# First network in eight tiles of three units instead of six of two and four of three

## The chip, the core and the metric

The kernel runs on one core of one Trainium2 chip. The metric is the device time of one launch in microseconds (us); lower is better. Engines are named as in the profile: PE (TensorE matmul), PEld (its weight loads), DVE (VectorE), ACT (ScalarE), POOL (GpSimd) and SP (SyncE, which issues the DMAs here).

## What is computed

Three stages follow each other. An attention with a complex decay runs over 4 batches, 8 heads, 768 steps and 48 channels; its output, put side by side over the heads, is a matrix of 3,072 tokens by 384, which passes through two feed-forward networks:

```
for t in range(S):                       # attention, per batch and head
    S_re, S_im = ar * S_re - ai * S_im + k[t] v[t]^T, ar * S_im + ai * S_re
    y[t] = q[t] @ S_re
g = x @ w_gate; x = (silu(g) * (x @ w_val)) @ w_out          # first network, 1,536 wide
h = x @ w_in;   out = (h - tanh(h)) @ w2_out                 # second network, 2,048 wide
```

## The kernel before

**Units and groups.** The tokens fall into 24 units of 128 (six per batch). Two units form a group. `group_steps` (L271) makes the decay powers of a group: its inputs are normed one group ahead (L224 to L250), turned by PE (`put_a`, L252), multiplied up in 14 steps of `cstep` (L262; three DVE instructions each, L266, L268, L269), copied to `NW` by ACT (L312, L313) and finished in L345 to L351. `unit_a` (L357) turns q and k of a unit, multiplies them with `NW` (L370, L376) and sends them through a DRAM scratch (`qk_d`, L378 to L383). `unit_b` (L402) makes the scores (L420), the masked scores (L423 to L426), the carried state (L432 to L441), the output (L446, L448) and the turned output, split into a high and a low part, `xh` and `xl` (L461 to L464).

**First network.** `moe1_tile` (L526) takes a tile of units. For each of 12 slices `f` of the width it makes the gate and the value products (L554, 18 products of the slice's weights with all columns of the tile), SiLU on ACT (L558), their product on DVE (L563), its split by ACT and POOL (L514, L515), and one slice later the output products (L538, nine of them). So a tile has 12 x 27 = 324 products, each as wide as the tile: 256 columns for two units, 384 for three. L523 loads a slice of `w_out` again for each tile after the first. A tile can start when `xh` and `xl` of its last unit are there.

**Order.** Ahead of the first tile the program runs the attention of the units of that tile (L682) and decodes the first ten weight slices (`dec1`, L184). Then, after each half slice of tile `ti`, `bg` (L715) advances the attention by `RATE` = 6 steps until the units of the next tile are done (L704), and during tile 0 also decodes the other 14 weight slices. In the last tile (L707) no attention is left; the second network's weights are decoded there. The second network (`moe2_tile`, L607) has its own tiles of three units. A scheduler then puts each engine's instructions into an order of its own, by a simulated timeline; on the chip an engine takes them in that order.

```
TILES = (2, 2, 2, 2, 2, 2, 3, 3, 3, 3)                  # L58
while prog["done"] < TILES[0] - 1:                      # L682
    att_next(TILES[0] - 1, SHARE0)
...
goal = sum(TILES[:ti + 2]) - 1                          # L704
```

Of the kernel before, what the change touches and what calls it, by code (L numbers as in the profile page):

```python
# [41 lines left out]
def tile_kernel(ctx: ExitStack, tc: tile.TileContext, q, k, v, a_re, a_im, w_gate, w_val, w_out, w2_in, w2_out, out):  # L42
# [12 lines left out]
    NF1 = FF1 // P  # L55
    NF2 = FF2 // P

    TILES = (2, 2, 2, 2, 2, 2, 3, 3, 3, 3)  # L58

    RAW, MID = 2, 3  # L60

# [4 lines left out]
    N_A, N0, W2STEP, LON = 6, 20, 2, 10  # L66
    TU = max(TILES)
    N_EARLY = 2
# [103 lines left out]
    def dec1_load():  # L172
        if len(raws) < len(dec1_jobs):
            kind, f = dec1_jobs[len(raws)]
            r = raw_p.tile([P, 2, DM], I64, tag="raw", name="raw", bufs=RAW)
            if kind == "o":
                ins = SP.dma_start(out=r[:, 0], in_=w_out[f * P:(f + 1) * P, :])
            else:
                for c, src in enumerate((w_gate, w_val)):
                    ins = SP.dma_start(out=r[:, c].rearrange("p (k c) -> p k c", k=NJ), in_=src[:, f * P:(f + 1) * P].rearrange("(k p) c -> p k c", p=P))  # L180
            raws.append(r)
            raw_ins.append(ins.ins)
# [213 lines left out]
    tile_u0 = []  # L396
    for ti, n in enumerate(TILES):
        tile_u0.append(len(unit_tile))
# [121 lines left out]
    def load_wo(n):  # L520
        if NF1 <= n < NF1 * len(TILES):
            t = m1.tile([P, 2, DM], F32R, tag="wo", name="wo", bufs=3)
            SP.dma_start(out=t.bitcast(F32), in_=wo_d[n % NF1])  # L523
            wo_t[n] = t

    def moe1_tile(ti, bg):  # L526
        x = xt.pop(ti)
        n_t = TILES[ti] * P
        tok = tile_u0[ti] * P
# [136 lines left out]
    def att_next(goal, share):  # L666
        prog["n"] += 1
        if prog["done"] < goal:
            if next(ustream, None) == "wait":
                next(gstream, None)  # L670
                return
        else:
            prog["more"] = max(prog["more"], 1.0)
        prog["more"] += share
        while prog["more"] >= 1:
            prog["more"] -= 1
            group_next()

    load_a(0)
    for i in range(RAW):  # L680
        dec1_load()
    while prog["done"] < TILES[0] - 1:  # L682
        att_next(TILES[0] - 1, SHARE0)
        if prog["n"] == QAT:
# [216 lines left out]
```

## Time and profile before

| | |
|---|---|
| median of 3 runs (range) | 1281.08 us (1279.9 to 1281.22) |
| profiled execution, its own time | 1280.44 us |
| its span, first to last instruction | 1278.7 us |
| mean granted TensorE clock | 0.943 |
| busy: PE, DVE, ACT, POOL | 1147.8, 1008.1, 695.3, 465.8 us |

The time is that of the whole launch, the span that of the program's instructions; 1.74 us lie around it. Clock 1.0 is 2.4 GHz, 0.5 is 1.2 GHz; a figure between is a mean over a stretch. Matmuls overlap on PE, so that what one costs in a run of them is the distance from start to start, not its duration. A stretch of the program is read by cutting the span where a tile's first SiLU (L558) starts.

### The profile page before, as it was taken

How to read it: one execution, taken by the hardware profiler on the slowest of the kernel's cores; microseconds unless marked ns; L12 is line 12 of the kernel's file. 1: busy time of each engine (PE TensorE's matmuls, PEld its weight loads, DVE VectorE, ACT ScalarE, POOL GpSimd, SP SyncE). 2: the span in 40 equal slices, each digit the busy share in tenths (PEclk: the TensorE clock that was granted, in tenths of full speed). 3: DMA queues.
4: the chain of work that ended last, by engine and by line, in shares of the span. 5: the costliest groups of instructions: out<-in, count | busy, mean ns of one | idle time of the engine just before them, and what ended most of it. 6: DMA issues, size and time to landing. Idle time of an engine off the chain costs nothing.

```text
span 1278.7 us, 21147 instructions
## 1 busy us (share of the span) xinstructions
PE 1147.8 (90%) x7512; PEld 1113.6 (87%) x7512; DVE 1008.1 (79%) x1961; ACT 695.3 (54%) x1454; POOL 465.8 (36%) x402
## 2 busy tenths in 40 slices
PE   3346899898999999999999998987999999999997
PEld 2126888898999998999999998877999999999996
DVE  6988988697675849677683328999998899999996
ACT  6454655556545463736534224446666566666664
POOL 0034454333252223233232224544444444444442
PEclk9755979999899999999999999998999999999999
DMA  6586667679676776768565546752101101101000
GB/s 169 141 203 146 145 185 194 158 194 215 158 176 178 183 186 151 184 155 185 160 145 141 147 118 221 235 173 87 57 1 57 38 20 56 38 19 56 1 19 22
DMA packets 282289, 163.53 MB, mean 128 GB/s; under 512 B 155328, under 2 KB 263232, under 8 KB 282176
## 3 DMA queue, kind: packets, MB, share of 16 engines
q1 hardware_dynamic: 282176, 162.10, 48.7%
q8 instruction: 61, 1.00, 0.3%
q14 instruction: 52, 0.43, 0.1%
HBM read 121.26 MB, written 37.86 MB: 124 GB/s over the span
## 4 chain that ended last, share of the span: by engine, by line
PE 53%; DVE 23%; ACT 8%; DMA 8%; issue 4%; POOL 2%; SPq 1%; DVEq 0%; ACTq 0%; POOLq 0%
PE l L617 14%; PE l L635 13%; PE l L554 12%; PE acc L538 5%; PE psS L420 2%; DVE prod L266 2%; DVE t L143 2%; DMA TQ<-qk_d 2%; PE psY L448 2%; DVE PL L268 2%; PE psY L446 2%; DVE t L142 1%; DVE t L583 1%; DVE t L144 1%; DMA raw<-in_moe_w_val_dram 1%
## 5 line engine op out<-in xcount | busy, mean ns | idle before, releaser
L515 POOL TENSOR_TENSOR lo<-t,hi 128x384 fp32r<-128x384 f32 (+1 forms) x247 | 289.4, 1172 | 517.2 <-ACT hi L514 485.7
L554 PE MATMUL l<-x,wgv 128*128 128x256 f32 (+1 forms) x2160 | 366.8, 317 | 21.6 <-DVE t L563 14.6
L554 PEld LDWEIGHTS l<-x,wgv 128*128 128x128 f32 x2160 | 324.4, 197 | 29.4 <-DVE t L563 19.4
L514 ACT CAST hi<-t 128x384 fp32r<-128x384 f32 (+1 forms) x248 | 119.5, 482 | 244.4 <-DVE t L563 141.6
L635 PE MATMUL l<-x,wi 128*128 128x384 f32 x1152 | 223.0, 339 | 8.3 <-DVE t L584 7.2
L635 PEld LDWEIGHTS l<-x,wi 128*128 128x128 f32 x1152 | 202.5, 189 | 9.9 <-DVE t L584 8.3
L617 PE MATMUL l<-w,hi 128*128 128x384 f32 x768 | 188.0, 338 | 0.5 <-ACT hi L514 0.5
L538 PE MATMUL acc<-hi,wo 128*128 128x256 f32 (+1 forms) x720 | 180.0, 312 | 4.0 <-ACT hi L514 2.7
L583 DVE SCALAR_TENSOR_TENSOR t<-vv,t 128x384 f32<-128x384 f32 x128 | 139.8, 1092 | 11.8 <-DVE t L582 0.5
L617 PEld LDWEIGHTS l<-w,hi 128*128 128x128 f32 x768 | 139.5, 189 | 0.8 <-ACT hi L514 0.8
L538 PEld LDWEIGHTS acc<-hi,wo 128*128 128x128 f32 x720 | 127.0, 193 | 5.8 <-ACT hi L514 3.8
L617 PE MATMUL l<-w,lo 128*128 128x384 f32 x384 | 120.2, 337 | 0.0
L563 DVE TENSOR_TENSOR t<-t,l 128x256 f32<-128x256 f32 (+1 forms) x120 | 56.2, 468 | 81.0 <-PE l L554 67.8
L538 PE MATMUL acc<-lo,wo 128*128 128x256 f32 (+1 forms) x360 | 111.3, 315 | 3.8 <-POOL lo L515 3.8
L266 DVE TENSOR_TENSOR prod<-PL 128x384 f32<-128x384 f32 x168 | 111.6, 664 | 3.1
L577 ACT ACTIVATE t<-l 128x384 f32<-128x384 f32 x128 | 62.9, 491 | 50.4 <-PE l L635 48.1
L579 DVE TENSOR_TENSOR l<-l,t 128x384 f32<-128x384 f32 x128 | 72.1, 563 | 13.1 <-ACT uu L578 13.1
L580 ACT ACTIVATE vv<-uu,gbias 128x384 f32<-128x384 f32 x128 | 79.4, 621 | 0.4
L558 ACT ACTIVATE t<-l 128x256 f32<-128x256 f32 (+1 forms) x120 | 51.1, 426 | 51.7 <-PE l L554 50.9
L584 DVE COPY_PREDICATED t<-far,l 128x384 f32<-128x384 int32 x128 | 75.8, 592 | 3.7
L446 PE MATMUL psY<-v,SC 128*128 128x48 f32 x384 | 75.3, 291 | 0.7 <-POOL SC L424 0.6
L538 PEld LDWEIGHTS acc<-lo,wo 128*128 128x128 f32 x360 | 69.2, 192 | 6.0 <-POOL lo L515 5.7
(131 smaller groups left out, 1936.8 us busy)
## 6 DMA issues: line engine op xcount, KB each, us to landing
wo<-wo_d SPq DMA_DIRECT2D x108, 384.0 KB, 3.9
qk_d<-QK SPq DMA_DIRECT2D x24, 768.0 KB, 4.6
raw<-in_moe_w_out_dram SPq DMA_DIRECT2D x28, 384.0 KB, 3.1
TK<-qk_d SPq DMA_DIRECT2D x48, 192.0 KB, 4.2
TQ<-qk_d SPq DMA_DIRECT2D x48, 192.0 KB, 5.1
x<-o_d SPq DMA_DIRECT2D x16, 576.0 KB, 5.2
raw<-in_moe_w_in_dram SPq DMA_DIRECT2D x16, 384.0 KB, 3.8
ar<-in_a_re_dram SPq DMA_DIRECT2D x24, 192.0 KB, 3.8
```

The costliest lines, as they stand in the source:

```text
L266: DVE.tensor_tensor(out=pr, in0=prev.unsqueeze(2).to_broadcast(sh), in1=cur.unsqueeze(1).to_broadcast(sh), op=ALU.mult)
L446: PE.matmul(o, lhsT=SC[h // 4][:, h % 4], rhs=vn[:, D * h:D * (h + 1)], start=True, stop=(c == 0))
L514: ACT.copy(out=hi, in_=t)
L515: eng.tensor_tensor(out=lo, in0=t, in1=hi.bitcast(F32), op=ALU.subtract)
L538: PE.matmul(acc[j], lhsT=w[:, a, j * P:(j + 1) * P], rhs=m[b], start=(f == 0 and i == 0), stop=(f == NF1 - 1 and i == 2))
L554: PE.matmul(p, lhsT=w[a][:, kk], rhs=x[b][:, kk, 0:n_t], start=(n == 0), stop=(n == 3 * NJ - 1))
L579: DVE.tensor_tensor(out=p, in0=p, in1=t, op=ALU.subtract)
L580: ACT.activation(out=vv, in_=uu, func=AF.Square, scale=1.0 / G_C, bias=gbias)
L583: DVE.scalar_tensor_tensor(out=t, in0=vv, scalar=G_F, in1=t, op0=ALU.add, op1=ALU.mult)
L584: DVE.copy_predicated(out=t, mask=far, data=p)
L617: PE.matmul(acc[tb], lhsT=g[a][:, tb * P:(tb + 1) * P], rhs=w2_hl[f][:, b], start=(f == 0 and n == 0), stop=(f == NF2 - 1 and n == 2))
L635: PE.matmul(p, lhsT=wi_hl[a][:, kk, sl], rhs=x[b][:, kk, :], start=(n == 0), stop=(n == 3 * NJ - 1))
```

## The change

```diff
-    TILES = (2, 2, 2, 2, 2, 2, 3, 3, 3, 3)
+    TILES = (3,) * 8
```

There are eight tiles of three units, where there were six of two and four of three. All first-network products have 384 columns: 2,592 of them (1,728 at L554, 864 at L538) where there were 3,240. L558 and L563 fall from 120 to 96, L514 and L515 by 24 each, the loads of L523 from 108 to 84. The attention and the second network have the same instructions as before. The loop at L682 runs three units, and tile `ti` is accompanied by the attention of three units.

On DVE the place is the end of the attention that stands ahead of tile 0's first product L563. Before, from the end of group 1 (`NW` L347 to L351; `x_586` is the low part of tile 0's input, here of unit 1):

```order
L347 SCALAR_TENSOR_TENSOR NW<-NW,x_840 128x768
...
L350 TENSOR_TENSOR NW<-NW,x_840 128x768
L351 SCALAR_TENSOR_TENSOR NW<-NW,x_840 128x768
L464 TENSOR_TENSOR x_586<-psX,x_585 128x3x128
L370 TENSOR_TENSOR qk<-psQ,NW 128x3x64
...
L376 TENSOR_TENSOR QK<-qk,NW 128x768
L563 TENSOR_TENSOR t<-t,l_871 128x256
```

Now, from the end of group 2 (`x_586` here is that of unit 2):

```order
L335 TENSOR_TENSOR lam<-lp 128x3x2
L347 SCALAR_TENSOR_TENSOR NW<-NW,x_1211 128x768
L464 TENSOR_TENSOR x_586<-psX,x_585 128x3x128
L350 TENSOR_TENSOR NW<-NW,x_1211 128x768
L351 SCALAR_TENSOR_TENSOR NW<-NW,x_1211 128x768
L435 TENSOR_TENSOR Z<-Hn,psG 96x384
L563 TENSOR_TENSOR t<-t,l_1149 128x384
```

All 14 steps of group 2 and its L347 stand ahead of unit 2's split L464 now; before, they stood behind the first L563, among the work of tile 0. Ahead of the first L563 DVE has 42 of L266 instead of 28, and the two L376 of unit 3 besides.

On PE the place is where the first products of tile 0 (L554, `x_585` the high part) begin. Before:

```order
L461 MATMUL psX<-ident,y 128x128 x3
L367 MATMUL psQ<-ident,q 128x128 x3
L256 MATMUL psA<-ident,ai 128x128 x3
L554 MATMUL l_806<-x_585,wgv_124 128x256
L554 MATMUL l_871<-x_585,wgv_124 128x256
```

Now:

```order
L420 MATMUL psS<-TQ,TK 128x128 x4
L256 MATMUL psA<-ident,ai 128x128 x3
L461 MATMUL psX<-ident,y 128x128 x3
L420 MATMUL psS<-TQ,TK 128x128 x4
L256 MATMUL psA<-ident,ar 128x128 x3
L554 MATMUL l_1074<-x_585,wgv_124 128x384
```

The scores of unit 3 (L420) stand ahead of the first product now; its state and output (L432, L446, L448) follow ten products later.

## Rows read from the trace of the kernel before

**Rows 1.** Busy time of the engines, span cut at each tile's first SiLU.
```profile
core 0: us, PE busy (x) PEld busy (x) DVE busy (x) ACT busy (x) POOL busy (x), PEclk, DMA share, GB/s
0.00:135.50 135.50, 63.56 (x249) 47.21 (x250) 107.17 (x223) 73.35 (x139) 32.29 (x30) 0.70 0.66 163
135.50:208.30 72.80, 65.49 (x495) 64.66 (x493) 62.52 (x127) 42.16 (x93) 35.90 (x33) 0.88 0.65 167
208.30:272.70 64.40, 59.21 (x479) 57.29 (x480) 51.79 (x113) 39.44 (x82) 24.26 (x23) 0.97 0.79 196
272.70:347.30 74.60, 66.85 (x538) 64.48 (x537) 56.54 (x129) 44.02 (x91) 26.41 (x26) 0.95 0.72 169
347.30:408.30 61.00, 59.15 (x497) 58.52 (x495) 42.60 (x96) 32.06 (x69) 22.35 (x20) 0.97 0.69 172
408.30:467.10 58.80, 54.88 (x470) 54.42 (x469) 41.81 (x94) 33.10 (x74) 17.68 (x17) 1.00 0.81 197
467.10:537.70 70.60, 66.34 (x545) 65.76 (x544) 51.81 (x120) 36.49 (x81) 21.34 (x23) 0.95 0.73 176
537.70:622.60 84.90, 83.09 (x549) 81.82 (x548) 67.46 (x145) 41.25 (x81) 29.08 (x23) 0.96 0.64 150
622.60:706.40 83.80, 83.61 (x558) 82.47 (x557) 45.48 (x99) 40.80 (x81) 23.61 (x22) 0.98 0.66 161
706.40:788.50 82.10, 81.00 (x532) 79.95 (x532) 34.12 (x58) 24.75 (x54) 23.56 (x24) 0.98 0.52 153
788.50:1278.70 490.20, 464.57 (x2621) 456.99 (x2619) 446.76 (x763) 287.84 (x616) 209.31 (x166) 0.99 0.19 63
```

**Rows 2.** Timeline of ACT (start, duration): the first SiLU of tile 0.
```profile
135.55 0.38 ACT L558 ACTIVATE t<-l 128x256 f32<-128x256 f32 x1
```

**Rows 3.** Timeline of DVE around the start of tile 0.
```profile
119.56 0.25 DVE L269 TENSOR_TENSOR PL<-prod 128x96 f32<-128x96 f32 x1
...
127.14 0.96 DVE L347 SCALAR_TENSOR_TENSOR NW<-NW,x 128x768 f32<-128x768 f32 x1
...
133.07 0.55 DVE L464 TENSOR_TENSOR x<-psX,x 128x384 fp32r<-128x384 f32 x1
...
137.59 0.56 DVE L266 TENSOR_TENSOR prod<-PL 128x384 f32<-128x384 f32 x1
```

**Rows 4.** Timeline of DVE: first L266 and last L269 of groups 3, 10, 11.
```profile
201.66 0.55 DVE L266 TENSOR_TENSOR prod<-PL 128x384 f32<-128x384 f32 x1
...
236.41 0.25 DVE L269 TENSOR_TENSOR PL<-prod 128x96 f32<-128x96 f32 x1
...
589.85 0.58 DVE L266 TENSOR_TENSOR prod<-PL 128x384 f32<-128x384 f32 x1
...
618.15 0.25 DVE L269 TENSOR_TENSOR PL<-prod 128x96 f32<-128x96 f32 x1
...
645.26 1.40 DVE L266 TENSOR_TENSOR prod<-PL 128x384 f32<-128x384 f32 x1
...
666.95 0.24 DVE L269 TENSOR_TENSOR PL<-prod 128x96 f32<-128x96 f32 x1
```

**Rows 5.** Timeline of PE: products of 256 and of 384 columns, scores.
```profile
476.42 1.24 PE L554 MATMUL l<-x,wgv 128*128 128x256 f32 x9
477.50 0.28 PE L538 MATMUL acc<-hi,wo 128*128 128x256 f32 x1
...
667.32 1.72 PE L554 MATMUL l<-x,wgv 128*128 128x384 f32 x9
668.88 0.33 PE L538 MATMUL acc<-lo,wo 128*128 128x384 f32 x1
...
669.22 1.95 PE L420 MATMUL psS<-TQ,TK 96*128 96x128 f32 x16
```

**Rows 6.** Who PE waited for in tiles 6 to 8: total, times, longest.
```profile
PE l L554 <- DVE t L563: 1.8, 1, 1.8
PE l L554 <- ACT t L558: 1.1, 1, 1.1
```

## The prediction

> **What bounds the kernel now.** I cut the span at each tile's first SiLU and read three things in each stretch: its length, how long PE was not busy, and the granted clock [rows 1]. The reader is to see four parts. Up to 135.5 us there is attention and weight decoding alone: DVE is busy for 107.17 us, PE for 63.56, at a clock of 0.70; PE is starved. The six tiles of two units take 402.2 us (537.7 - 135.5) with 13 units of attention, and PE stands idle in them for 30.3 us (72.80 - 65.49 in tile 0, then 5.2, 7.8, 1.9, 3.9, 4.3). The next three tiles, of three units and three units of attention each, take 250.8 us, and PE idles for 3.1: here PE is the bound, and it waits for another engine but twice, 2.9 us in all [rows 6]. From 788.5 us on there is the last tile and the second network, 490.2 us. Per unit of tokens that is 33.5 us in a tile of two and 27.9 in a tile of three. This gap is what the change reaches for, and the first part is what it lengthens.
>
> **What falls out.** The tail of 490.2 us has the same instructions and, PE's last 2,368 instructions among them, the same order at its end: nothing. Tiles 6 to 8 of before become tiles 4 to 6 and keep their units; by PE's counts in the new order they carry 0.5 us less: -0.5. The 24 dropped loads of L523, and 24 each of L558, L563, L514 and L515, lie beside PE's products on ACT, POOL, SP and DVE; I cost them at nothing by themselves, since PE is what I count, and where that cover fails it is in the idle time below. So the question is one sum: units 0 to 11 of the first network end at 537.7 us now; they will end at **S + t0 + t1 + t2 + t3**, with S the first SiLU of tile 0 and four tiles of three.
>
> **S, the later start.** Now S is 135.55 [rows 2]. In the new order unit 2's split L464 stands on DVE behind all of group 2's steps and its L347. Group 2's first L266 runs at 137.59 [rows 3], and up to there little changes. How long its 14 steps take without first-network work beside them the trace doesn't show. Groups with the same instructions took 34.8 us (group 3, 201.66 to 236.41) and 28.3 (group 10), and group 11, which has no norm of a later group in it, 21.7 [rows 4]. Group 10 is nearest; less some 3 us of first-network work on DVE I take 25. From the last L269 to L347 it took 7.6 us in group 1 (119.56 to 127.14), where ACT had more to do; I take 6. L347 needs 1 us, and from L464 to the first SiLU it was 2.5 us (133.07 to 135.55) [rows 2, 3]. So S = 137.6 + 25 + 6 + 1 + 2.5 = **172**, 36.5 later. The ends: 21.7 and 5 us give 167.9, 34.8 and 7.6 give 183.5. What stands behind the waiting L464 on DVE are L350, L351 and L563, and on PE behind the first ten products the state and output of unit 3: all wait with it, but unit 3 is due only in tile 1.
>
> **The tiles of three.** The base is tile 7 of before: 83.8 us, PE idle for 0.2, clock 0.98 [rows 1]. I correct it by what PE's new order has more or fewer of, at 0.173 us for a product of 384 columns (nine in 1.56 us) and about 0.11 for a score, output or transpose, where a score or an output is two instructions on the chip [rows 5].
> t3: 4 products fewer, 12 transposes and 2 scores more: +1.1; 1 us of idle as in tiles 6 to 8: **86**.
> t1: 6 products, 21 transposes and 4 scores more: +4.3; 1 us idle: **89**.
> t2: 24 products fewer, 9 transposes and a few small ones more: -1.2. DVE carries the most here after tile 0, by its counts a tenth more than tile 6, in which it was busy for 67.46 of 84.90 us. I add 4 us of idle, between 0.2 and 7.8 (tiles 7 and 2 of before), and 2.5 for a clock of 0.95 as in tile 2: **89**.
> t0: 24 products fewer, the rest nearly even: -4.2, so 79.6 us of PE at 0.98. Tile 0 ran at 0.88, which makes 88.6, and idled for 7.3; I take 4.4 of that: **93**. Bounds: DVE decodes 14 slices here; its count is 1.23 times that of before, so 77 us for 62.52, and with the 10.3 us that the old tile 0 took beyond its DVE, 87. The high end is 96.
>
> The sum is 172 + 93 + 89 + 89 + 86 = 529, against 537.7: -8.7, with the -0.5 **-9.2**. The profiled execution took 1280.44 us, so 1271.2; the median of the runs is 0.64 higher, so **1272** us.
> The break-even is an average of 91.4 us a tile, (537.7 - 172) / 4.
>
> How much of this is the wider product alone? Nine products of 256 columns take 1.08 us and nine of 384 take 1.56 [rows 5]. Units 0 to 11 have 1,944 of the first or 1,296 of the second: 233.3 or 224.6 us, 8.7 less. That is inside the 27.9 us per unit. The Trainium skill, TensorE: Matmul & The Clock Gate, section Back-to-back issue gap, gives a gap of the columns at 2.4 GHz and some 2.5 ns more, so 109.2 and 162.5 ns. [...] The trace doesn't agree at either width (120 and 173 ns), and it has both in this kernel, so I go by it.
>
> **The rivals.**
> *The attention sets the pace of the early tiles (slower).* Its mechanism: DVE and the round trips through DRAM deliver a unit of attention each 30.9 us in tiles 0 to 5 (402.2 / 13), and wider tiles don't change that. Tiles 0 to 3 need 12 units: 371 us, above the 365.7 from which it decides. Then 172 + 371 = 543, +5.3 - 0.5, so 1286. For it: DVE is busy for 62.52 of 72.80 us in tile 0 and 51.79 of 64.40 in tile 1, and the early idle time recurs. Against: tiles 3 and 4 went at 30 with DVE at 70%, tiles 6 and 7 at 28, and unit 3 and group 2 are nearly done before tile 0 begins.
> *The start is later than 172.* If group 2 goes at group 3's pace, S is 183.5; with the tiles as forecast, 1283.
> *Tiles as clean as 6 to 8 (faster).* S at 168, t0 at 87, the others 85, 83.5 and 84 with hardly a wait: 507.5, so 1250.
> *Tile 0 at a low clock (slower).* The lengthened stretch ahead has PE as thin as before, at 0.70. If tile 0 ran at 0.70 as well, its 79.6 us would take 111, 18 more: 1290. Against: with the wide products that follow each other there, tile 0 has less reason to pause than the old one, which had 0.88. The Trainium skill, same page, section The HAM clock gate, says the clock is held at half until the PE has been busy; by that rule the start of tile 0 is slow in either version, and the trace agrees so far as it shows 0.70 ahead of the products and 0.88 with them [rows 1].
>
> That the change would not do what it says I leave out: the new order has 384 columns throughout.
>
> **How the numbers follow.** Forecast 0.46, attention's pace 0.25, late start 0.10, clean tiles 0.14, low clock 0.05. A measurement tells about 0.2% from no change, so 1278.5 to 1283.6 is the same. S and t0 together move the forecast by some 6 us either way, so it is not faster throughout. Faster: clean tiles 0.14, forecast 0.42, late start 0.02, together 0.58. The same: forecast 0.04, late start 0.05, the low end of attention's pace 0.07, together 0.16. Slower: attention's pace 0.18, late start 0.03, low clock 0.05, together 0.26. The range runs from 1256, which leaves the lower half of the clean tiles out, to 1291, which takes in the low clock's 1290 and leaves out only a worse pace of attention than 30.9.
>
> **What would show it.** Right: first SiLU of tile 0 at 168 to 176 us; tile 0 at 90 to 96 us; tiles 1 to 3 under 90 each with PE idle for under 5; tiles 4 to 6 within 2 us of 84.9, 83.8, 82.1; 490 us from there. Wrong: a first SiLU after 180; tiles 1 to 3 above 93 with PE waiting for DVE or DMA; a granted clock below 0.85 in tile 0; any change of the last stretch beyond 2 us.

## The result and the profile after

| | before | changed |
|---|---|---|
| median of 19 runs each (range) | 1281.22 us (1274.67 to 1287.81) | 1287.58 us (1281.95 to 1293.07) |
| ratio of the runs, 95% interval | | 1.0053 (1.0036 to 1.0069) |
| profiled execution: its own time, span | 1280.44, 1278.7 us | 1287.81, 1286.1 us |
| mean granted TensorE clock | 0.943 | 0.933 |

The changed kernel is 0.5% slower; 1272 us were forecast, 0.7% less than before. Runs of the same kernel lie up to 13 us (1%) apart, so that differences of this size are read from the ratios, and a profile of one execution shows where time went rather than how much to a microsecond.

Busy time of the changed kernel by engine, its span cut at each tile's first SiLU, as in [rows 1]:

```profile
0.00:175.20 175.20, 89.97 (x361) 69.45 (x361) 139.79 (x293) 90.77 (x175) 44.76 (x39) 0.64 0.64 153
175.20:268.20 93.00, 84.60 (x523) 79.88 (x523) 71.31 (x143) 50.82 (x103) 44.49 (x33) 0.95 0.55 138
268.20:368.20 100.00, 92.13 (x607) 88.59 (x607) 71.50 (x147) 53.86 (x108) 34.80 (x29) 0.98 0.70 164
368.20:455.80 87.60, 82.18 (x545) 80.28 (x544) 73.12 (x159) 42.47 (x84) 28.79 (x21) 0.98 0.64 154
455.80:547.90 92.10, 88.97 (x577) 86.44 (x576) 65.00 (x127) 55.28 (x108) 30.52 (x25) 0.94 0.66 159
547.90:633.10 85.20, 84.31 (x550) 82.86 (x549) 62.88 (x143) 37.25 (x76) 26.27 (x21) 0.96 0.63 154
633.10:714.10 81.00, 81.00 (x558) 80.42 (x557) 46.75 (x100) 40.92 (x81) 21.05 (x22) 1.00 0.67 164
714.10:796.90 82.80, 80.33 (x538) 79.23 (x537) 33.59 (x59) 25.28 (x55) 23.65 (x24) 1.00 0.54 154
796.90:1286.10 489.20, 464.84 (x2621) 456.85 (x2619) 447.05 (x763) 288.56 (x616) 208.54 (x166) 0.99 0.19 63
```

Laid against the sum of the prediction:

| us | before | forecast | measured |
|---|---|---|---|
| first SiLU of tile 0 (S) | 135.5 | 172 | 175.2 |
| first network of units 0 to 11 | 402.2 | 357 (93, 89, 89, 86) | 372.7 (93.0, 100.0, 87.6, 92.1) |
| units 12 to 20 | 250.8 | 250.3 | 249.0 |
| last tile and second network | 490.2 | 490.2 | 489.2 |
| span | 1278.7 | 1269.5 | 1286.1 |

The span is 16.6 us above the sum, 11.0 of them in tile 1 and 6.1 in tile 3; the other terms, of which the start is 3.2 over, nearly cancel. PE idles in the four early tiles for 8.4, 7.9, 5.4 and 3.1 us (length less PE busy), 24.8 in all; the forecast had 10.4. In the later three it idles for 3.4, close to the 3.1 of [rows 1].

The chain to the first SiLU answers to [rows 3]. From the timeline of DVE: group 2's last L269, its L347, and unit 2's split. From that of PE: tile 0's first ten products, and what follows them.

```profile
163.97 0.25 DVE L269 TENSOR_TENSOR PL<-prod 128x96 f32<-128x96 f32 x1
...
169.16 0.96 DVE L347 SCALAR_TENSOR_TENSOR NW<-NW,x 128x768 f32<-128x768 f32 x1 [2.42 <-ACT x L346]
171.87 0.56 DVE L464 TENSOR_TENSOR x<-psX,x 128x384 fp32r<-128x384 f32 x1 [1.76 <-ACT x L463]
```

```profile
171.89 3.05 PE L554 MATMUL l<-x,wgv 128*128 128x384 f32 x10 [0.21 <-ACT x L463]
174.78 1.48 PE L432 MATMUL psG<-v,Kn 128*96 128x48 f32 x16
```

The start was sized well. What stands out is the attention behind it. The timeline of DVE, L464 (a unit's split, the end of its attention) of units 5 and 6, first in the kernel before:

```profile
268.15 0.55 DVE L464 TENSOR_TENSOR x<-psX,x 128x384 fp32r<-128x384 f32 x1
...
296.33 0.56 DVE L464 TENSOR_TENSOR x<-psX,x 128x384 fp32r<-128x384 f32 x1
```

and in the changed one:

```profile
256.90 0.55 DVE L464 TENSOR_TENSOR x<-psX,x 128x384 fp32r<-128x384 f32 x1
...
308.23 0.56 DVE L464 TENSOR_TENSOR x<-psX,x 128x384 fp32r<-128x384 f32 x1 [0.85 <-ACT x L463]
```

Unit 5 is 11 us earlier than before the change. Unit 6, which came 28 us behind unit 5, now comes 51 behind it, and is 12 us later than before. The lead that the late start gave the attention is lost there. In DVE's order unit 6 begins at the very end of tile 0. In the program's order its group 3 is advanced in tile 0 only once unit 5 is done (`SHARE1` = 0 at L63 and L730), since no unit of tile 0's goal needs it; and unit 6's first half (`unit_a`) runs along with unit 5's second half only where group 3 is done by then (L488 to L494), and is otherwise left to tile 1. Below, "the hold" is this setting. The scheduler moves group 3's steps forward all the same, so that the group itself is ready in time; it is unit 6 that waits. The last instruction of group 3's `NW` (L351) and the first L376 of unit 6:

```profile
244.70 1.64 DVE L351 SCALAR_TENSOR_TENSOR NW<-NW,x 128x768 f32<-128x768 f32 x1
...
267.74 0.95 DVE L376 TENSOR_TENSOR QK<-qk,NW 128x768 f32<-128x768 f32 x1
```

### The profile page after: what moved, and what is told of

The parts are those of the page before. It is cut to its first block, busy times and chain, and to the rows that moved or that the text cites. A ratio compares the mean times of both kernels' runs of the same rounds, so it can differ in the third digit from the quotient of the medians.

```text
span 1286.1 us, 19615 instructions
## 1 busy us (share of the span) xinstructions
PE 1148.3 (89%) x6864; PEld 1104.0 (86%) x6864; DVE 1011.0 (79%) x1931; ACT 685.2 (53%) x1396; POOL 462.9 (36%) x378
## 4 chain that ended last, share of the span: by engine, by line
PE 53%; DVE 27%; ACT 8%; DMA 5%; issue 4%; SPq 1%; POOL 1%; DVEq 0%; ACTq 0%; POOLq 0%
PE l L635 14%; PE l L617 14%; PE l L554 12%; PE acc L538 5%; DVE prod L266 4%; DVE PL L268 3%; DVE t L143 2%; DVE PL L269 2%; PE psS L420 2%; DMA raw<-in_moe_w_val_dram 2%; DVE QK L376 2%; DVE t L563 1%; PE psY L446 1%; DVE t L142 1%; PE psY L448 1%
## 5 line engine op out<-in xcount | busy, mean ns | idle before, releaser
L515 POOL TENSOR_TENSOR lo<-t,hi 128x384 fp32r<-128x384 f32 x223 | 281.0, 1260 | 515.9 <-ACT hi L514 489.9
L554 PE MATMUL l<-x,wgv 128*128 128x384 f32 x1728 | 356.1, 350 | 20.1 <-DVE t L563 14.1
L554 PEld LDWEIGHTS l<-x,wgv 128*128 128x128 f32 x1728 | 305.9, 194 | 28.8 <-DVE t L563 20.2
L514 ACT CAST hi<-t 128x384 fp32r<-128x384 f32 x224 | 115.1, 514 | 255.5 <-DVE t L563 149.6
L538 PE MATMUL acc<-hi,wo 128*128 128x384 f32 x576 | 167.4, 343 | 0.9 <-DVE x L544 0.9
L583 DVE SCALAR_TENSOR_TENSOR t<-vv,t 128x384 f32<-128x384 f32 x128 | 139.1, 1087 | 11.8 <-DVE t L582 0.5
L538 PEld LDWEIGHTS acc<-hi,wo 128*128 128x128 f32 x576 | 107.1, 192 | 1.9 <-DVE x L544 1.5
L266 DVE TENSOR_TENSOR prod<-PL 128x384 f32<-128x384 f32 x168 | 106.1, 632 | 3.0
L538 PE MATMUL acc<-lo,wo 128*128 128x384 f32 x288 | 100.4, 349 | 2.5 <-POOL lo L515 2.4
L563 DVE TENSOR_TENSOR t<-t,l 128x384 f32<-128x384 f32 x96 | 52.6, 548 | 63.3 <-PE l L554 50.6
L577 ACT ACTIVATE t<-l 128x384 f32<-128x384 f32 x128 | 62.9, 491 | 47.7 <-PE l L635 45.2
L420 PE MATMUL psS<-TQ,TK 96*128 96x128 f32 x384 | 57.7, 302 | 25.3 <-DMA TQ<-qk_d 23.9
L420 PEld LDWEIGHTS psS<-TQ,TK 96*128 96x128 f32 x384 | 54.3, 215 | 28.1 <-issue 24.1
L446 PE MATMUL psY<-v,SC 128*128 128x48 f32 x384 | 73.2, 286 | 1.2 <-POOL SC L424 1.2
```

Of the source, the lines that this page charges most:

```text
L266: DVE.tensor_tensor(out=pr, in0=prev.unsqueeze(2).to_broadcast(sh), in1=cur.unsqueeze(1).to_broadcast(sh), op=ALU.mult)
L420: PE.matmul(ps[:, P * i:P * (i + 1)], lhsT=TK[:, 4 * hh + i], rhs=TQ[:, 4 * hh + i], start=True, stop=True)
L446: PE.matmul(o, lhsT=SC[h // 4][:, h % 4], rhs=vn[:, D * h:D * (h + 1)], start=True, stop=(c == 0))
L514: ACT.copy(out=hi, in_=t)
L515: eng.tensor_tensor(out=lo, in0=t, in1=hi.bitcast(F32), op=ALU.subtract)
L538: PE.matmul(acc[j], lhsT=w[:, a, j * P:(j + 1) * P], rhs=m[b], start=(f == 0 and i == 0), stop=(f == NF1 - 1 and i == 2))
```

## Experiments

The two parts of the change can be had singly, since a tile's width can be set alone. Each of the following carries one edit; ratios are to the kernel before, run beside it.

**The late start alone, with as many two-unit tiles as before.**

```diff
-    TILES = (3,) * 8
+    TILES = (3, 2, 2, 2, 2, 2, 2, 3, 3, 3)
```

> Tiles (3, 2, 2, 2, 2, 2, 2, 3, 3, 3): as many tiles of two as before, but the first tile waits for three units. Theory 'start': the first SiLU is 40 us later (about 175 us), of which some 12 us of attention on PE come ahead of it; the products of two units cost what they did, so the rest stays lost, and the time is about 1300 us, well above the changed kernel's 1287. Rival 'pace': the attention's pace sets when units 0 to 11 are through whatever the widths and the start are; the time is within 3 us of the changed kernel's, 1284 to 1290.

Measured: 1307.27 us, 1.0229 (1.0206 to 1.0252). Its stretches up to the first tile, and of two of the two-unit tiles:

```profile
0.00:175.50 175.50, 93.06 (x371) 71.81 (x371) 139.44 (x293) 90.54 (x175) 45.37 (x39) 0.64 0.64 152
...
324.00:390.20 66.20, 61.47 (x514) 60.40 (x514) 53.14 (x111) 37.43 (x77) 25.78 (x23) 0.97 0.71 171
390.20:458.90 68.70, 61.05 (x519) 59.64 (x517) 48.30 (x107) 31.97 (x70) 21.05 (x21) 1.00 0.68 167
```

The start is at 175.5 as in the changed kernel, and the time is 2.3% above the kernel before: some 29 us are lost of the 40 by which the start moved. The six two-unit tiles take 65.3 us in the mean, hardly less than those of before (67.0). The rival, by which the attention's pace sets the end whatever the start and the widths are, falls: it gave 1284 to 1290. From here to the changed kernel only the two-unit tiles go, and with them 1.8%, some 22 us. So, with the hold as it is, the change is a loss of about 29 us and a gain of about 22. How much of the 29 is the hold's was not measured: no run has these tiles without it.

**Some of the width alone, the start as before.**

```diff
-    TILES = (3,) * 8
+    TILES = (2, 2, 2, 3, 3, 3, 3, 3, 3)
```

> Tiles (2, 2, 2, 3, 3, 3, 3, 3, 3): start as before, but units 6 to 11 in two tiles of three. Theory 'start' (the late start lost what the width won): first SiLU at 135.5 us as before; tiles 3 to 5 of before (190.4 us for six units) become two of some 87 us, less an attention unit that falls to the next tile: 5 to 10 us less than before, 1271 to 1276. Rival 'pace': the attention's units come when they came before, and so does the end: 1279 to 1283.

Measured: 1271.90 us, 0.9942 (0.9922 to 0.9962): 7.4 us less than before, as the theory of the start has it. Its tiles 3 and 4 take 177.5 us, where tiles 3 to 5 of before took 190.4 [rows 1]:

```profile
358.30:444.40 86.10, 85.01 (x570) 83.27 (x569) 73.09 (x158) 42.25 (x82) 29.05 (x21) 0.98 0.67 161
444.40:535.80 91.40, 87.43 (x578) 83.93 (x577) 65.55 (x128) 55.19 (x108) 31.36 (x25) 0.98 0.68 163
```

**More tiles of two, late in the program.**

```diff
-    TILES = (2, 2, 2, 2, 2, 2, 3, 3, 3, 3)
+    TILES = (2, 2, 2, 2, 2, 2, 2, 2, 2, 3, 3)
```

> Tiles (2 x 9, 3, 3): the kernel before with units 12 to 17 in three tiles of two instead of two of three, start as before. If a two-unit tile costs through its gaps beside the attention also late: three at 60 to 64 us instead of 84.9 + 83.8, 10 to 20 us above the kernel before. If the wider products alone count (1,944 of 120 ns for 1,296 of 173 ns in twelve units, so 4.4 us in six): 3 to 6 us above.

Measured: 1299.66 us, 1.0138 (1.0116 to 1.0160). Its tiles 6 to 8, of two units each:

```profile
531.60:592.90 61.30, 57.74 (x484) 56.94 (x482) 44.58 (x96) 31.74 (x69) 20.65 (x20) 0.97 0.69 168
592.90:665.50 72.60, 65.76 (x497) 64.77 (x497) 39.45 (x94) 33.08 (x73) 20.32 (x20) 0.88 0.67 161
665.50:730.80 65.30, 61.98 (x506) 61.34 (x505) 38.43 (x93) 26.03 (x61) 18.58 (x20) 0.95 0.65 161
```

The loss of 17.7 us by the ratio is four times what the narrower products cost by themselves (4.4 us). The three tiles take 199.2 us, where the two tiles of three that stood there took 168.7; tile 5 ahead of them is 7 us shorter than before (63.6), since the attention of one unit passes from it to them. Gaps and the clock have a part in the rest: PE idles for 3.6, 6.8 and 3.3 us at a clock down to 0.88, against 1.8 and 0.2 us at 0.96 and 0.98 [rows 1]. DVE isn't seen to cause it: in the longest of the three tiles it is busy for 39.45 of 72.60 us, and PE's waits there are put down to POOL (2.8 us), DMA (2.0) and ACT (2.0), none to DVE.

**Groups released in tile 0.** In the changed kernel:

```diff
-    SHARE0, SHARE1, SHARE, RATE = 1, 0, 2.0, 6
+    SHARE0, SHARE1, SHARE, RATE = 1, 2.0, 2.0, 6
```

> The changed kernel with SHARE1 = 2 instead of 0, so that groups go on during tile 0's attention and unit 6 (which followed unit 5 by 51 us instead of 28) can begin in tile 0. If that lost lead made tile 1 take 100 us: unit 6's split about 10 us earlier, tile 1 near 90 us, time about 1278. If it is PE's own work and the gaps of a busy DVE and ACT: tile 0 longer by what tile 1 loses, time 1285 to 1290.

Measured: 1274.98 us, 0.9974 (0.9957 to 0.9990), so 0.8% under the changed kernel and 0.3% under the kernel before. On its timeline of DVE, the first L376 of unit 6, and the splits of units 5 and 6:

```profile
244.03 0.94 DVE L376 TENSOR_TENSOR QK<-qk,NW 128x768 f32<-128x768 f32 x1
...
264.19 0.55 DVE L464 TENSOR_TENSOR x<-psX,x 128x384 fp32r<-128x384 f32 x1
...
296.48 0.56 DVE L464 TENSOR_TENSOR x<-psX,x 128x384 fp32r<-128x384 f32 x1 [2.75 <-ACT x L463]
```

and its first five stretches:

```profile
0.00:174.60 174.60, 89.08 (x363) 67.81 (x364) 138.44 (x293) 91.05 (x176) 42.80 (x39) 0.65 0.64 153
174.60:271.70 97.10, 89.70 (x550) 87.63 (x550) 81.10 (x159) 52.99 (x106) 43.91 (x35) 0.91 0.62 152
271.70:365.60 93.90, 88.57 (x584) 84.94 (x583) 68.87 (x151) 57.31 (x111) 32.01 (x29) 0.98 0.66 157
365.60:449.10 83.50, 82.20 (x542) 81.39 (x541) 64.32 (x141) 37.37 (x75) 23.47 (x20) 0.96 0.64 158
449.10:539.10 90.00, 87.34 (x573) 85.01 (x571) 64.81 (x129) 55.43 (x107) 34.21 (x25) 0.96 0.69 166
```

Unit 6 begins 23.7 us earlier, in tile 0, and its split is 11.8 us earlier. Tile 0 takes 4.1 us more with 9.8 us more of DVE work in it, tile 1 takes 6.1 less, tile 2 4.1 and tile 3 2.1; PE idles for 16.7 us in the four instead of 24.8, and is busy for as long (347.8 us, against 347.9). The start is the same. So about two thirds of the miss, 0.8% of some 1.2%, go with the hold.

**The hold made longer.** In the changed kernel, in the program's order, no group advances in tile 0 once units 3 to 5, which it accompanies, are done:

```diff
+        elif prog.get("hold"):
+            return
         else:
             prog["more"] = max(prog["more"], 1.0)
...
         prog["credit"] = 0.0
+        prog["hold"] = ti == 0
```

> The changed kernel with the groups held in tile 0 altogether once its three units are done (with the change they went on then), so that unit 6 begins after tile 0's end. If the hold of group 3 costs by delaying unit 6: unit 6's split later than 308 us, and 2 to 8 us above the changed kernel, 1289 to 1296. If it was another difference in the order that made SHARE1 = 1 and 2 faster: 1275 to 1289, without regard to when unit 6 comes.

Measured: 1298.63 us, 1.0123 (1.0101 to 1.0145), 0.7% above the changed kernel, some 9 us where 2 to 8 were expected. Units 5 and 6:

```profile
261.62 0.56 DVE L464 TENSOR_TENSOR x<-psX,x 128x384 fp32r<-128x384 f32 x1 [0.96 <-ACT x L463]
...
324.27 0.55 DVE L464 TENSOR_TENSOR x<-psX,x 128x384 fp32r<-128x384 f32 x1
```

and its tile 1:

```profile
269.40:378.90 109.50, 98.15 (x601) 93.96 (x600) 83.39 (x172) 62.02 (x124) 33.45 (x29) 0.91 0.70 170
```

With unit 6 behind unit 5 by 32, 51 and 63 us, tile 1 takes 93.9, 100.0 and 109.5 us, and the ratio is 0.9974, 1.0053 and 1.0123. So the hold is shown as a cause, in both directions. The two edits don't act by the same path, though. Here it is group 4 that moves: its first L266 is at 281.9 us, in tile 1, instead of 252.3, and DVE is busy for 83.4 us in tile 1 instead of 71.5. And in its profile the loss is not in PE's idle time (22.6 us in the four tiles, against 24.8) but in a longer busy time at a lower clock, 0.90 and 0.91 in tiles 0 and 1, where the changed kernel had 0.95 and 0.98.

**A smaller release.** `SHARE1` = 1:

> The changed kernel with SHARE1 = 1. In DVE's order unit 6 still begins after tile 0's end, as with 0. If SHARE1 = 2 helped by letting unit 6 begin in tile 0, this does nothing: 1284 to 1290, unit 6 about 50 us behind unit 5. If any progress of the groups in tile 0 helps: 1274 to 1281.

Measured: 1282.23 us, 0.9998 (0.9979 to 1.0018), 0.55% or some 7 us under the changed kernel. Neither expectation holds: the median lies between their ranges. Unit 6's split, and tile 1:

```profile
304.97 0.56 DVE L464 TENSOR_TENSOR x<-psX,x 128x384 fp32r<-128x384 f32 x1
```

```profile
267.20:362.70 95.50, 89.76 (x596) 85.96 (x596) 69.08 (x144) 53.05 (x109) 32.36 (x29) 0.98 0.69 166
```

Unit 6 still comes 49 us behind unit 5, 3 us earlier than in the changed kernel, and still begins in tile 1; yet most of the gain of `SHARE1` = 2 is there (its interval, 0.9957 to 0.9990, overlaps this one). So a unit 6 that comes late is not shown to be how the hold costs; what else in the scheduler's order does it stays open.

**The same release in the kernel before.**

> The kernel before with SHARE1 = 2, nothing else. Unit 4 followed unit 3 by 49 us there. Theory 'held group in a wide tile 0': the two-unit tiles lose little by the hold, since tile 0 is short and holds two units; the time stays at 1278 to 1282. Rival 'general': the hold costs both kernels alike, and the time falls by the 12 us that it cost the changed kernel, to 1266 to 1271, so that the change as such costs 6 to 7 us with either setting.

Measured: 1285.36 us, 1.0026 (1.0010 to 1.0041). It does not gain there, it loses a little, 3 us above what was expected. Unit 4 does come sooner, 32 us behind unit 3 instead of 49, and tile 2 takes 66.2 us for 74.6; but tile 0 takes 80.7 for 72.8, with PE idle for 15.0 us instead of 7.3. So of the two kernels only the one with a tile 0 of three units gains by the release. With `SHARE1` = 2 in both, the change is worth about -0.5% (0.9974 to 1.0026); with 0 in both, +0.5%.

**The masks of the first eight units.** `SCM = 0` in the changed kernel:

> The changed kernel with SCM = 0: the scores of units 0 to 7 are masked by DVE in one step (L426) as those of the others, not by an ACT copy and a POOL select. If the idle of PE in tiles 0 and 1 (16 us) comes from these two in the chain: idle near 8 us, time about 1280. If it comes from DVE being late: 1.4 us more DVE work a unit makes it the same or worse, 1287 to 1292.

Measured: 1292.45 us, 1.0094 (1.0068 to 1.0119). That is 0.4% above the changed kernel, with intervals that just touch, so the masks on ACT and POOL are not what makes it slow. The reason that was expected for it isn't shown: PE's idle time in tiles 0 and 1 does fall, from 16.3 to 12.0 us, but tile 0 runs at a clock of 0.84 instead of 0.95 and takes 100.7 us instead of 93.0.

**Two versions more.** Tiles (2, 2, 2, 3, 3, 3, 3, 3, 3) with `SHARE1` = 2:

> Tiles (2, 2, 2, 3, 3, 3, 3, 3, 3) with SHARE1 = 2. If the gain of fewer two-unit tiles (7.6 us) and that of SHARE1 add: 1260 to 1268. If SHARE1 only mends what a tile 0 of three units breaks: 1270 to 1274.

Measured: 1273.85 us, 0.9931 (0.9905 to 0.9957). The gains don't add; the interval covers the ratio of the same tiles with `SHARE1` = 0 (0.9942). Tiles (2, 3, 3, 3, 3, 3, 3, 2, 2) with `SHARE1` = 2:

> Tiles (2, 3, 3, 3, 3, 3, 3, 2, 2) with SHARE1 = 2: as many three-unit tiles as in (2, 2, 2, 3, ...), but the early tile only at the start, and the two others last. If the early start is what counts and two-unit tiles cost alike anywhere: within 4 us of tiles (2, 2, 2, 3, ...) with SHARE1 = 2. If two-unit tiles cost more among the early attention than late: 5 us or more below it. If the last tile of two covers the second network's weights too little: more than 5 us above.

Measured: 1288.76 us, 1.0043 (1.0022 to 1.0064), 14 us or more above the former. Whether it is the last tile of two or the two-unit tile ahead of it was not tried apart, and its tile 0, of two units beside the attention of three, is a third place: it takes 107.2 us, with PE idle for 21.7. The tiles (2, 2, 2, 3, 3, 3, 3, 3, 3) beat both kernels, with the start of the one and half of the other's wide tiles.

## Why the prediction was wrong

- **S** (172, measured 175.2) held. Group 2's 14 steps took 24.6 us (139.36 to 163.97) where 25 were taken, L347 came 5.2 us behind them (6). Against these 1.2 us stand 1.8 for a later first L266, 1.8 in which L464 waited for ACT's L463, and 0.9 from L464 to the first SiLU, where the first ten products took 2.9 us from start to start instead of some 1.7. The granted clock was 0.66 from 172.0 to 175.2 us, between its two levels of 1.2 and 2.4 GHz, and 1.00 from there to 200; up to 175.2 PE was busy for 89.97 us only. The Trainium skill, TensorE: Matmul & The Clock Gate, section The HAM clock gate, has the clock at half until PE has been busy. The trace agrees: 289 ns a product there, and 173 ns at the full clock [rows 5]. That tile 0 starts slow "in either version" is not so, however: in the kernel before, the clock was 1.00 from 133 to 150 us.
- **The late start's price** was implied, not named: 36.5 us less the attention done ahead. Measured with two-unit tiles behind it and the hold left in, it is some 29 us.
- **t0 and t2** (93 and 89, measured 93.0 and 87.6), units 12 to 20 (-0.5, measured -1.8; singly 85.2, 81.0 and 82.8 us for 84.9, 83.8 and 82.1) and the tail (0, measured -1.0) held. So the wide tile does take 27.7 us a unit late in the program, close to the 27.9 of [rows 1]. That t0 came out to the tenth is luck: PE was busy for 84.6 us at a clock of 0.95 where 88.6 at 0.88 were taken, and idle for 8.4 where 4.4 were. In t2 too PE idled for more than was taken (5.4 us for 4.2), and the low clock that was taken, 0.95, did not occur (0.98).
- **t1 and t3 are the step that failed**: "1 us idle" in each. t1 took 100.0 us for 89, 6.9 of it PE idle beyond the 1 us, the other 4.1 PE busy beyond the base and the +4.3, which no run explains. t3 took 92.1 for 86: 2.1 of it PE idle beyond the 1 us, the other 4.0 PE busy, at a clock of 0.94 where the base had 0.98 (by that ratio some 3.6 us, an estimate). The step took tiles 6 to 8 of before as the pattern for any tile of three, as if their cleanness came from their width. It comes from their place as well: of eight tiles of one width, PE idles for 24.8 us in the first four and for 3.4 in the next three. What the early place costs is in part the hold: without it PE idles for 16.7 us in the four, and the time is 0.8% less. Why the rest of the early idle time is there was not tried. The prediction used the order of the new kernel only for PE's counts and for what stands ahead of the first product; that unit 6 begins at the end of tile 0 is in it too.
- **The rivals.** Attention's pace gave 1286, next to the result, and its sum for units 0 to 11 (371 us) is next to the 372.7 measured; but its mechanism, a pace of 30.9 us a unit that no tile can beat, does not stand: with the same late start and two-unit tiles the time is 1307, with `SHARE1` = 2 it is 1275, and tiles 4 and 5 of the changed kernel take 28.4 and 27.0 us a unit with three units of attention each. PE is busy for 347.9 of the 372.7 us, so that waits for the attention can be 24.8 us of them at most. A number that fits was no proof. The late start at group 3's pace (183.5) did not occur. The low clock in tile 0 did not either: it was 0.95, above the old tile's 0.88. (The price of that rival was reckoned too low: 111 us for 93 leaves out the 4.4 us of idle time that the 93 hold, so that it would have come to some 1294.) The clean tiles came only late.
- **The width** was right in sign and too low in size where it was reckoned by products alone: twelve units in wide tiles are worth some 22 us, of which 8.7 are the products. The sum, by whole tiles, had it at 45.2 (402.2 less 357), which took in the attention moved ahead, and got 29.5.

## What to carry to other kernels

A tile that is cheap late in a program is not cheap early: before a tile's cost is carried to another place, see what feeds it there, and in which order the feeders are released. A change of tile size moves every point that is tied to a tile's end; here a setting that cost nothing with two units held up the attention with three, and had to be changed with it. Of the tiles tried here the best had three narrow ones first, which keep the early start, and wide ones from where the pipeline is filled (0.9942 and 0.9931); wide tiles throughout gave 1.0053, and 0.9974 once the release was changed with them.

## What was not expected

Two-unit tiles late in the program cost far more than their narrower products say, even where DVE is busy for 54% of the time (39.45 of 72.60 us): 17.7 us for three of them in place of two wide ones, where products account for 4.4. And a small change of the release (`SHARE1` 0 to 1), which moves unit 6 by 3 us only, moved the time by 0.55%: with an order made by a scheduler, a difference of half a per cent can hang on details of the order that the profiles read here don't name.
